# Four more units with states in quarters: a planned stage of an mLSTM and MLP kernel is re-planned

## The chip, the cores and the metric

The kernel runs on one core of a Trainium2 chip. The metric is the time of one execution on the device in microseconds; the median over the runs counts. A profile comes from a separate execution, which has a time of its own.

## The reference, cut to what matters

An mLSTM cell runs over 768 tokens for 4 batches of 8 heads with 40 features each; its output, seen as 3072 tokens of 320 features, goes through an MLP with 2048 hidden units and the activation h - tanh(h).

```python
m_new = np.maximum(f_gate[:, :, t] + m, i_gate[:, :, t])
f_stab = np.exp(f_gate[:, :, t] + m - m_new)
i_stab = np.exp(i_gate[:, :, t] - m_new)
C = f_stab * C + i_stab * einsum('bhd,bhe->bhde', vt, kt)
n = f_stab * n + i_stab * kt
h_tilde = einsum('bhde,bhe->bhd', C, qt)
denom = np.maximum(np.abs(einsum('bhd,bhd->bh', n, qt)), 1.0)
y[:, :, t] = o * h_tilde / denom        # o = sigmoid(o_gate)
...
h = x @ w_in
g = h - np.tanh(h)
return g @ w_out
```

## The kernel before

**Units and items.** The cell's work is cut into 24 units: unit n is 128 tokens (chunk c = n // 4) of batch b = n % 4, all 8 heads. Two units make a group of 256 tokens for the MLP (12 groups). The MLP's hidden units are cut into 8 pairs of 128-wide blocks; (group, pair) is the MLP's step, and an item is two such steps. On TensorE an item has 12 products ph_up (x times w_in) and then, one item later, the products with w_out: either 8 `po` products, or, where the group or the pair is number 4 or later, 7 products per step instead of 8 (`pS`, in `down_seven`; the names "runs of seven products" and "third bank" belong to it). `sums_of_g` and `sums_of_weights` make the sums that the seven products need, and `put_together` adds the results up on VectorE.

**A unit, in trios.** Scores (`ps`) are k times q for each head; the mask makes P of them, on VectorE (TENSOR_TENSOR P) or, for the units in BY_POOL, by a copy on ScalarE and an affine_select on GpSimd. `vs` are the values scaled by the input gate, with a column of the gate itself. `ph` is then the state of the chunk before times q (three products over trios of heads, from a second layout of q, `q2`) plus P times vs (eight products, P as the weights). `gate` divides by the denominator and multiplies by the sigmoid; three transposes on TensorE (`px`) and a copy bring y into `xT`, in which the MLP reads it. `update` (`pc`, three products) and `keep_state` make the new state.

**A unit, in quarters.** Units from 12 on hold the state in two halves of 64 rows. `block_turned` computes the result transposed, P streaming past the values (`pT`: 8 products with the state, 8 with P, into quarters of two banks), and 8 small state products (`pc`, 64x41). The result comes back by a trip through DRAM: `turn_back` transposes 32x32 blocks on VectorE (`zt`), stores them (4 DMAs `h_rows`) and loads them (4 DMAs `z_in`); `gate_turned` makes y; `turn_by_store` transposes blocks again (`yt`), stores (4 DMAs `y_rows`) and loads into xT (2 DMAs). All of these DMAs are on SP's queue. `in_halves` carries a state from trios to halves with small DMAs SBUF to SBUF.

**Weights.** They arrive as float64 bits; `weights` fetches a block with DMAs on GpSimd's queue and converts it: two ops on VectorE (`parts`), two on ScalarE (`low`, `power`), then `one`, `sign` and `product` on VectorE.

**What sets the order.** The class Pinned and T keep each engine's instructions in the order in which the program calls them. For units 0 to 11 and the items up to START this order comes from `Plan`: a list scheduler over engines with estimated durations, buffers as tokens, ranks, earliest times (`at`) and lags; where TensorE would idle, it puts in filler products (`awake`, lines of `stream`). After the plan a loop merges the rest: each item's products with the slots of units 12 to 23. Between the two stands `load_unit(PLANNED, ("kz", "qz", "v", "k", "o"))`, unit 12's loads on SP; in the kernel before, the in_halves of the four batches come right behind it. Line L129 of the profile is the helper that records TensorE's products, L133 its transposes, L106 the helper of all other engines.

Of the kernel before, what the change touches and what calls it, by code (L numbers as in the profile page):

```python
# [60 lines left out]
L = 128  # L61
# [18 lines left out]
def kernel(  # L80
# [76 lines left out]
    class Plan:  # L157
# [5 lines left out]
        COLD, TURN, WAIT = (6.2, 1.8), 0.12, 0.2188  # L163
# [346 lines left out]
    def weights(dst, srcs, queue):  # L510
# [41 lines left out]
        def product():  # L552
            V.tensor_tensor(out=dst, in0=w["r"], in1=w["e"].bitcast(FP), op=OP.mult)
# [5 lines left out]
    def blocks_of(p):  # L559
# [9 lines left out]
        for i in range(2):  # L569
            whole.append((slice(i * HALF, (i + 1) * HALF), slices(4, 1), moe_w_in[half[i]:half[i] + HALF, slices(2 * p + i, 1)]))  # L570
        return (weights(w_in[:, p, :], whole, G),
                weights(w_out[:, 2 * p:2 * p + 2, :].rearrange("p two n -> p (two n)"),
                        [(every, slice(0, 2 * DM), moe_w_out[slices(2 * p, 2), :].rearrange("(two p) n -> p two n", two=2))], G))
# [40 lines left out]
    def scaled(n, i, name, bufs, by_heads=False):  # L614

        t = un[n]
        flat = att.tile([L, H * D1 + HALF - D1], FP, name=name, tag=name, bufs=bufs)
        to = flat[:, 0:H * D1].rearrange("p (h d) -> p h d", d=D1)
        t["wide"] = flat
        scale = ei[:, i, t["c"], t["hs"]]  # L620
        t["column"] = lambda: A.copy(out=to[:, :, D], in_=scale)
        if by_heads:
            for h in range(H):
                A.mul(out=to[:, h, 0:D], in_=t["v"][:, h], mul=scale[:, h:h + 1])
        else:
            V.tensor_tensor(out=to[:, :, 0:D], in0=t["v"], in1=scale.unsqueeze(2).to_broadcast([L, H, D]), op=OP.mult)
        return to
# [107 lines left out]
    def turn_by_store(n):  # L735
# [6 lines left out]
        V.transpose(flat[:, 0:NK * 128], y[:, 0:NK * 128])  # L742
        V.transpose(flat[:, NK * 128:], y[:, FROM[NK]:])
        rows = dram.tile([(NK + 1) * 128, L], FP, name="y_rows", tag=f"y_rows{n % 4}")
        for a in range(L // BLOCK):
            part = slice(a * BLOCK, (a + 1) * BLOCK)
            SP.dma_start(out=rows[:, part].rearrange("(b i) j -> i b j", i=BLOCK), in_=yt[part])
        for i in range(2):
            half = slice(i * HALF, (i + 1) * HALF)
            SP.dma_start(out=xT[g % NX][half, :, tt * L:(tt + 1) * L], in_=rows.rearrange("(c p) t -> p c t", p=128)[half])  # L750

    def in_halves(b):


        old, new = (state[b][i].rearrange("p h d -> p (h d)") for i in (1, 0))
        for h in (0, 1, 2, 4, 5, 6, 7):
            i, j = divmod(h, HH)
            r = h % TRIO
            n = 2 if h == 0 else 1
            to, at = (x[:, first * D1:(first + TRIO * (n - 1) + 1) * D1].rearrange("p (h d) -> p h d", d=D1)[:, ::TRIO]  # L760
                      for x, first in ((new, j), (old, h)))
            SP.dma_start(out=to[i * HALF:i * HALF + D], in_=at[r * D:(r + 1) * D])

    def block_turned(n):
# [4 lines left out]
        G.memset(t["wide"][:, H * D1:], 0.0)  # L769
# [31 lines left out]
    def turn_back(n):  # L801
# [5 lines left out]
        for i in range(2):  # L807
            V.transpose(flat[:, i * 2 * L:(i + 1) * 2 * L], t["turned"][i].rearrange("p g t -> p (g t)"))
        rows = dram.tile([2, 2, HH, L, BLOCK], FP, name="h_rows", tag=f"h_rows{n % 4}")
        for a in range(128 // BLOCK):  # L810
            half, low = divmod(a, 2)
            SP.dma_start(out=rows[low, half].rearrange("g (b k) i -> k (g b) i", k=BLOCK), in_=zt[a * BLOCK:(a + 1) * BLOCK])
        t["z"] = att.tile([L, 2, H, BLOCK], FP, name="z_in", tag="P", bufs=4)
        for i in range(4):
            part = slice(i * BLOCK, (i + 1) * BLOCK)
            SP.dma_start(out=t["z"][part].rearrange("t a h i -> t (a h) i"),
                         in_=rows.rearrange("a c g t i -> t (a c g) i")[part])
# [27 lines left out]
    def cell_slot(s, o):  # L845
# [16 lines left out]
        steps.append((0.0, lambda: turn_by_store(o)))  # L862
# [303 lines left out]
    SCALED, SHARED = (7, 11), (3, 5, 7, 8, 9, 10, 11)  # L1166
    RANKS = (-1.0, -1.0, -8.2006, -8.4463, 6.0242, 2.3893, 9.5327, 2.6415, 25.6922, 13.6176, 29.7021, 7.061)
    WEIGHTS = (0.08, -0.3563, 5.1266, 7.6972, 9.6586, 11.6503, 11.1391, 25.4848)
    START = item(FIRST * NP)
    HOLD = 43.9795  # L1170
    FETCH = {(0, 1): 6.75, (2, 1): 12.25, (3, 0): 19.87, (3, 1): 31.49}
    APART = ()
    BY_POOL = (2, 5, 6, 7, 8, 9)
# [56 lines left out]
    LATE = {"o": -2.69, "k": -3.541, "q2": -4.0692, "v": -1.3038}  # L1230

    def plan_unit(n, rank):
# [17 lines left out]
        else:  # L1250
# [3 lines left out]
            if c:  # L1254
# [14 lines left out]
        u["scores"] = plan.add("T", 1.0, first_part, [u["qz"], *(of(n - 2, "second") if n in (2, 3) else [])], rank, [(bank, held), ("P", held)], tiles=2, hold=HOLD * (n // B), dense=0.4 if n else 0.6)  # L1269
        if n in BY_POOL:  # L1270
            copies = [plan.add("A", 0.55, lambda i=i: ready[1][i][0](), [u["scores"]], rank - 6.4275, give=[(bank, held)] if i else ()) for i in range(2)]
            u["mask"] = [plan.add("G", 0.9, lambda i=i: ready[1][i][1](), [copies[i]], rank + 2.098, lag=0.1) for i in range(2)]
        else:
            u["mask"] = [plan.add("V", 0.62, lambda i=i: ready[1][i](), [u["scores"]], rank - 1.673, give=[(bank, held)] if i else ())
                         for i in range(2)]
        before = of(n - B, "state")
# [4 lines left out]
        op = None  # L1281

        def second_part(j, heads):
            banks[:] = [held["small"]]
            inter(n, j)
            for h in heads:
                intra(n, h)

        parts = TRIOS if c else [range(i * HH, (i + 1) * HH) for i in range(2)]
        for j, heads in enumerate(parts):  # L1290
            op = plan.add("T", 0.223 * len(heads) + (0.22 if c else 0.0), lambda j=j, heads=heads: second_part(j, heads),
                          ([op] if op else [u["prep"], u["column"], *before, *of(n, "q2") * (c > 0)]) + (u["mask"] if c else u["mask"][j:j + 1]), rank,
                          take=() if op else [("small", held)], give=[("P", held)] if j == len(parts) - 1 else (), dense=0.32)
        u["second"] = op
        if shared:
            steps = []
            over = plan.add("V", 0.6, lambda: [steps.extend(gate(n, in_parts=True)), steps[0]()], [op], rank - 0.2851)
            shares = plan.add("A", 1.9, lambda: steps[1](), [over, u["open"]], rank + 9.0221)
            u["gate"] = plan.add("V", 0.5, lambda: steps[2](), [shares, *of(n - 2, "turn")], rank - 7.2476, give=[("small", held)])
        else:  # L1300
            u["gate"] = plan.add("V", 1.6, lambda: gate(n), [op, u["open"], *of(n - 2, "turn")], rank, give=[("small", held)])

# [7 lines left out]
        def turns():  # L1310
            banks[:] = [held_x["small"]]
            for j in range(NK + 1):
                turn(n, j, at_once=False)

        u["turn"] = plan.add("T", 0.35, turns, [u["gate"]], rank, [("small", held_x)], dense=0.5)
        u["x"] = plan.add("A", 0.5, lambda: keep_x(n), [u["turn"]], rank + 1.345, give=[("small", held_x)])
        late = rank + (3.0653 if c else -10.0273)
        u["update"] = plan.add("T", 0.64, updates, [u["second"], u["k"]], late, [("small", held_c)], [("vs", held)],
                               at=0.0 if c else 0.0 if n < 2 else 50.4842, dense=0.5)
        u["state"] = plan.add("V", 1.0 if c else 0.5, lambda: keep_state(n), [u["update"], *before, *of_states[c]], late, give=[("small", held_c)])  # L1320
# [3 lines left out]
    def plan_weights(p, rank, at):  # L1324
        for k, block in enumerate(blocks_of(p)):
            fetch, parts, low, power, one, sign, product = block
            held, r, buffer = {}, rank + 4.428 * k, "w64" + "ab"[k]
# [7 lines left out]
            converted[p, k] = plan.add("V", 0.75, product, [op] + (of_tokens[NT - 1] + of_states[NT - 1] if p >= KEPT else []), r, give=[("w", held)])  # L1335
# [7 lines left out]
    for n in range(2, PLANNED):  # L1343
        if n == 2 * B:
            plan_gates(1, 8.7699, 30.0, in_po)
# [6 lines left out]
    for p in range(SPLIT, NP):  # L1352
        steps = []
        op = None
        for i in range(2):
            op = plan.add("V", 0.65, lambda p=p, i=i, steps=steps: [steps.extend([] if i else sums_of_weights(p)), *[step() for _, step in steps[2 * i:2 * i + 2]]],
                          [op] if op else [converted[p, 1], *([made[p - 1]] if p % 2 else [converted[n, k] for n in range(1, NP) for k in range(2)])], -7.7512 + -3.8283 * p)
        made[p] = op

    def plan_item(x):  # L1360
# [35 lines left out]
        for i in range(2):  # L1396
            z.append(plan.add("A", 0.3 + 0.25 * n, lambda i=i: square(i), [op, *z], -1.1546, () if i else [("z", held), ("gt", held)]))
        q = [plan.add("A", 0.2 + 0.25 * n, lambda i=i: got[2][1](i), [z[i]], -7.0688) for i in range(2)]
        cube = [plan.add("V", 0.15 + 0.27 * n, lambda i=i: got[2][2](i), [z[i]], -8.4237, give=[("up", held)] if i else ()) for i in range(2)]
        g = [plan.add("V", 0.15 + 0.27 * n, lambda i=i: got[2][3](i), [q[i], cube[1]], -17.7698, give=[("z", held)] if i else ()) for i in range(2)]  # L1400
        shrunk = g
        seven, (group, pair) = in_seven(*some[0]), some[0]
        if seven:
            g = [plan.add("V", 0.8 * n, lambda: sums_of_g(some), g[-1:], 4.1746, [("w", held), ("s4", held)])]
# [315 lines left out]
```

## Time and profile before

| what | value |
|---|---|
| median of 3 runs | 521.77 us (521.42, 521.77, 532.6) |
| the profiled execution: time | 523.67 us |
| the profiled execution: span | 522.0 us |
| mean granted TensorE clock | 0.995 |
| TensorE busy | 512.8 us, 98% |
| VectorE, ScalarE, GpSimd busy | 368.4, 200.6, 38.3 us |
| scores of unit 12 begin on TensorE | 209.71 us |

The lines of the profile name an engine (PE is TensorE, DVE VectorE, ACT ScalarE, POOL GpSimd, SPq the queue of SyncE), a line, an operation, what it writes and reads by the program's names, and how often. Times in the timeline and in the chain are microseconds from the start of the span: first the start, then the length of the stretch. In the chain a stretch lasts until the next one begins; in the timeline it lasts until its last instruction's end.

### The profile page before, as it was taken

Reading aid. Unit: us, or ns where it says so; the run is one execution under the profiler, and the core shown is the slowest. Engines: PE = TensorE matmul, PEld = TensorE weight load, DVE = VectorE, ACT = ScalarE, POOL = GpSimd, SP = SyncE. Lnnn points to the kernel's source line nnn. Section 1 sums busy time; section 2 is a strip of 40 time slices with the busy share of each in tenths; the row PEclk is TensorE's granted clock in tenths of the full one; section 3 lists DMA queues with packets and bytes.
Section 4 is the critical chain, followed back from the end, with each engine's and each line's share of the span. In section 5 each row is a group of like instructions: output and inputs, shape, how many; then the busy total and the mean of one; then the engine's idle time right before and its main releaser. Section 6 shows DMA issues by size and latency. Waiting matters only on the chain.

```text
span 522.0 us, 9917 instructions
## 1 busy us (share of the span) xinstructions
PE 512.8 (98%) x3705; PEld 442.4 (85%) x3705; DVE 368.4 (71%) x828; ACT 200.6 (38%) x511; POOL 38.3 (7%) x75
## 2 busy tenths in 40 slices
PE   9999999999999999999999999999999999999995
PEld 5778888887898888898898898898888888898984
DVE  5899979998855657786767667668658658663734
ACT  4465697676434242231321331232232232232321
POOL 5423224120000000000000000000000000000000
PEclk9899999999999999999999999999999999999999
DMA  7987646431003000042533533534433432310001
GB/s 228 285 245 227 180 141 193 131 111 33 3 3 91 6 27 26 4 108 50 133 64 89 147 67 85 129 69 87 107 77 85 107 79 36 80 31 1 26 1 31
DMA packets 100383, 47.29 MB, mean 91 GB/s; under 512 B 75048, under 2 KB 94056, under 8 KB 100328
## 3 DMA queue, kind: packets, MB, share of 16 engines
q1 hardware_dynamic: 94096, 31.84, 25.3%
q0 software_dynamic: 3040, 10.82, 6.6%
q10 hardware_dynamic: 3192, 3.93, 2.2%
q8 instruction: 31, 0.51, 0.4%
q14 instruction: 24, 0.20, 0.1%
HBM read 36.91 MB, written 9.44 MB: 89 GB/s over the span
## 4 chain that ended last, share of the span: by engine, by line
PE 94%; DMA 3%; ACT 1%; POOL 1%; DVE 0%; issue 0%; SPq 0%; DVEq 0%
PE ph_up L129 42%; PE pS L129 31%; PE po L129 7%; PE ph L129 4%; PE pT L129 4%; PE ps L129 4%; PE pc L129 2%; DMA w<-in_moe_w_in 2%; PE px L133 1%; DMA w_out<-in_i_gate 0%; POOL w L106 0%; ACT vs L106 0%; PE awake L129 0%; ACT L106 0%; DVE w_in L106 0%
## 5 line engine op out<-in xcount | busy, mean ns | idle before, releaser
L129 PE MATMUL ph_up<-xT,w_in 128*128 128x256 f32 (+1 forms) x1152 | 228.9, 388 | 0.0
L129 PEld LDWEIGHTS ph_up<-xT,w_in 128*128 128x128 f32 (+1 forms) x1152 | 176.2, 189 | 35.5 <-issue 15.3
L106 ACT ACTIVATE z<-ph_up 128x512 f32<-128x512 f32 (+1 forms) x98 | 56.8, 583 | 254.2 <-issue 123.7
L106 DVE SCALAR_TENSOR_TENSOR gt<-ph_up,z 128x512 f32<-128x512 f32 (+1 forms) x98 | 63.5, 675 | 68.0 <-ACT z L106 67.6
L129 PE MATMUL pS<-wT,s 128*128 128x160 f32 x480 | 72.0, 299 | 0.0
L129 PEld LDWEIGHTS pS<-wT,s 128*128 128x128 f32 x480 | 67.4, 190 | 0.0
L106 ACT ACTIVATE q<-z,tiny 128x512 f32<-128x512 f32 (+1 forms) x98 | 66.3, 711 | 1.0
L106 DVE SCALAR_TENSOR_TENSOR gt<-q,gt 128x512 f32<-128x512 f32 (+1 forms) x98 | 63.2, 676 | 0.0
L106 DVE TENSOR_TENSOR P<-ps,upto 128x512 f32<-128x512 f32 x36 | 23.3, 686 | 52.9 <-PE ps L129 52.8
L129 PE MATMUL pS<-w_out,gt 128*128 128x160 f32 x320 | 54.3, 312 | 0.0
L129 PEld LDWEIGHTS pS<-w_out,gt 128*128 128x128 f32 x320 | 44.6, 189 | 7.5 <-issue 3.6
L129 PE MATMUL po<-w_out,gt 128*128 128x320 f32 x128 | 38.2, 441 | 0.0
L129 PEld LDWEIGHTS po<-w_out,gt 128*128 128x128 f32 x128 | 23.1, 190 | 8.5 <-issue 0.3
L106 DVE TENSOR_TENSOR s<-gt 128x256 f32<-128x256 f32 x80 | 30.2, 418 | 0.0
L129 PE MATMUL pS<-w_out,s 128*128 128x160 f32 x160 | 28.3, 299 | 0.0
L129 PE MATMUL pS<-wT,gt 128*128 128x160 f32 x160 | 28.3, 299 | 0.0
L129 PEld LDWEIGHTS ps<-qz,kz 40*128 40x128 f32 x384 | 25.7, 190 | 2.1 <-issue 0.7
L129 PE MATMUL ps<-qz,kz 40*128 40x128 f32 x384 | 26.5, 276 | 0.0
L129 PEld LDWEIGHTS ph<-vs,P 128*128 128x128 f32 x192 | 23.9, 192 | 1.6 <-POOL P L106 1.2
L129 PE MATMUL ph<-vs,P 128*128 128x41 f32 x192 | 24.4, 273 | 0.7 <-POOL P L106 0.7
L129 PEld LDWEIGHTS pS<-w_out,s 128*128 128x128 f32 x160 | 23.9, 190 | 0.0
L129 PEld LDWEIGHTS pS<-wT,gt 128*128 128x128 f32 x160 | 23.9, 190 | 0.0
(105 smaller groups left out, 475.6 us busy)
## 6 DMA issues: line engine op xcount, KB each, us to landing
w<-in_moe_w_out POOLq DMA_DIRECT2D x8, 640.0 KB, 6.2
w<-in_moe_w_in POOLq DMA_DIRECT2D x16, 256.0 KB, 4.7
kz<-in_kT SPq DMA_DIRECT2D x48, 80.0 KB
o<-in_o_gate SPq DMA_DIRECT2D x24, 160.0 KB
k<-in_k SPq DMA_DIRECT2D x20, 180.0 KB
qz<-in_qT SPq DMA_DIRECT2D x44, 80.0 KB
v<-in_v SPq DMA_DIRECT2D x22, 160.0 KB
out<-ob ACTq DMA_DIRECT2D x11, 320.0 KB
```

The lines of the kernel that those rows point to most:

```text
L106: i = method(*args, **kwargs)
L129: return cls.keep(nc.tensor.matmul(*args, **kwargs))
L133: return cls.keep(nc.tensor.transpose(*args, **kwargs))
```

## The change

Units 8 to 11 (FLIPPED) are also computed in quarters, inside the plan: the trips through memory become steps of the plan (`turn_back` and `turn_by_store` now return three steps, blocks, stores and loads). `in_halves` moves into the plan, before each of these units, and carries eight pieces from state 0 to state 1 instead of seven from 1 to 0. The memset of vs's tail goes from GpSimd to VectorE and is done in `scaled`. Five weight products (ONE_BY_POOL) go to GpSimd. The third bank of the seven-product runs of groups 0 and 2 moves to the small banks (IN_SMALL). All ranks, earliest times, fetch times and the lists SCALED, SHARED, BY_POOL and APART are new. The load of unit 12 stays behind the plan.

```diff
-    def weights(dst, srcs, queue):
+    def weights(dst, srcs, queue, by_pool=False):
...
-            V.tensor_tensor(out=dst, in0=w["r"], in1=w["e"].bitcast(FP), op=OP.mult)
+            (G if by_pool else V).tensor_tensor(out=dst, in0=w["r"], in1=w["e"].bitcast(FP), op=OP.mult)
...
+        if n in FLIPPED or n >= PLANNED:
+            V.memset(flat[:, H * D1:], 0.0)
...
     def in_halves(b):
-        old, new = (state[b][i].rearrange("p h d -> p (h d)") for i in (1, 0))
-        for h in (0, 1, 2, 4, 5, 6, 7):
+        old, new = (state[b][i].rearrange("p h d -> p (h d)") for i in (0, 1))
+        for h in range(H):
...
+            SP.dma_start(out=new[i * HALF:i * HALF + D, j * D1:(j + 1) * D1], in_=old[r * D:(r + 1) * D, h * D1:(h + 1) * D1])
...
     def block_turned(n):
         t = un[n]
-        G.memset(t["wide"][:, H * D1:], 0.0)
...
-    SCALED, SHARED = (7, 11), (3, 5, 7, 8, 9, 10, 11)
+    SCALED, SHARED = (7, 10), (3, 4, 5, 9, 10)
...
-    FETCH = {(0, 1): 6.75, (2, 1): 12.25, (3, 0): 19.87, (3, 1): 31.49}
-    APART = ()
-    BY_POOL = (2, 5, 6, 7, 8, 9)
+    FETCH = {(2, 1): 18.26, (3, 0): 18.54, (3, 1): 38.13}
+    APART = (2,)
+    FLIPPED = (8, 9, 10, 11)
+    FLIPS = (3.0955, -4.5081, 2.7967, 0.1482, -2.8187, -1.6309)
+    SCORED = {4: 26.61, 6: 23.58, 8: 98.4, 9: 133.43, 10: 139.01, 11: 78.31}
+    ONE_BY_POOL = ((0, 1), (2, 1), (3, 0), (5, 1), (6, 1))
+    IN_SMALL = (0, 2, 3)
+    BY_POOL = (2, 5, 6, 9, 11)
...
+        if n in FLIPPED:
+            before = [plan.add("S", 2.8, lambda: in_halves(b), of(n - B, "state"), rank + FLIPS[5])]
+        else:
+            before = of(n - B, "state")
...
+            u["second"] = plan.add("T", 1.9, products, [u["prep"], u["column"], *u["mask"], u["k"], *before], rank + FLIPS[0], [("a", banked), ("small", held_c)], [("P", held), ("vs", held)], tiles=3, dense=0.9)
+            blocks = plan.add("V", 0.75, lambda: [backs.extend(turn_back(n)), backs[0]()], [u["second"]], rank + FLIPS[1], [("P", turned)], [("a", banked)])
+            u["update"] = u["state"] = plan.add("V", 0.5, lambda: keep_halves(n), [u["second"], *of_states[c]], rank + FLIPS[2], give=[("small", held_c)])
+            stores = plan.add("S", 2.1, lambda: backs[1](), [blocks], rank - 0.5, give=[("P", turned)])
+            loads = u["loads"] = plan.add("S", 2.1, lambda: backs[2](), [stores], rank - 0.5, [("P", back)])
+            both = plan.add("V", 1.0, lambda: [gates.extend(gate_turned(n)), *[step() for step in gates[:2]]], [loads, u["open"], *of(n - 2, "turn")], rank + FLIPS[3])
+            u["gate"] = plan.add("V", 0.6, lambda: [step() for step in gates[2:]], [both], rank + FLIPS[3], give=[("P", back)])
+            u["turn"] = plan.add("V", 0.65, lambda: [turns_y.extend(turn_by_store(n)), turns_y[0]()], [u["gate"]], rank + FLIPS[4])
+            stores = plan.add("S", 2.1, lambda: turns_y[1](), [u["turn"]], rank - 0.5)
+            u["x"] = plan.add("S", 1.3, lambda: turns_y[2](), [stores], rank - 0.5)
...
-            name = "small" if group == FIRST - 1 else "a"
+            name = "small" if group in IN_SMALL else "a"
...
+    plan.add("T", 0.0, lambda: None, [units[n]["x"] for n in (FIRST * GT, FIRST * GT + 1)], 1000.0)
...
     load_unit(PLANNED, ("kz", "qz", "v", "k", "o"))
-    for b in range(B):
-        in_halves(b)
```

## The prediction, made before the changed kernel was run

> **What bounds the kernel now.** I read the page first: how full TensorE is, and whose time the chain that ended last consists of.
>
> ```profile
> span 522.0 us, 9917 instructions
> PE 512.8 (98%) x3705; PEld 442.4 (85%) x3705; DVE 368.4 (71%) x828; ACT 200.6 (38%) x511; POOL 38.3 (7%) x75
> ...
> PE 94%; DMA 3%; ACT 1%; POOL 1%; DVE 0%; issue 0%; SPq 0%; DVEq 0%
> ```
>
> TensorE is the bound, and nearly nothing else is on the path. So two things count: how many microseconds of products the change takes off TensorE, and whether it makes TensorE wait. For the first I read the chain in order of time (start, duration, what). Fp32 products have two records each, transposes one.
>
> ```profile
> 56.94 0.65 PE px L133 x6
> ...
> 130.52 1.72 PE ph L129 x16
> ...
> 133.18 0.60 PE ph L129 x6
> 133.77 0.67 PE pc L129 x6
> ...
> 205.19 4.52 PE ph_up L129 x24
> 209.71 0.89 PE ps L129 x16
> 210.60 4.00 PE pS L129 x28
> ...
> 219.12 1.62 PE pT L129 x32
> 221.19 4.00 PE pS L129 x28
> ```
>
> The three rows from 130 us are unit 11 as it is now; the row at 56.94 is the turning of two units' results. A unit in quarters (from 219.12) has its block products and then its small state products until the next row at 221.19: 2.07 us. Between 205 and 215 one sees that TensorE goes from one group to the next without a gap: the scores of unit 12 start at 209.71, the moment the 24 records before them end.
>
> For the second I read the queue that a unit in quarters needs, SP's issues in order of time, which stand behind each other in one order:
>
> ```profile
> 164.53 0.87 SPq L106 DMA_DIRECT2D kz<-in_kT  x2
> ...
> 225.63 1.98 SPq L106 DMA_DIRECT2D h_rows<-zt  x4
> 229.09 1.90 SPq L106 DMA_DIRECT2D z_in<-h_rows  x4
> 231.03 0.80 SPq L106 DMA_DIRECT2D kz<-in_kT  x2
> 231.88 0.69 SPq L106 DMA_DIRECT2D qz<-in_qT  x2
> ...
> 242.04 1.90 SPq L106 DMA_DIRECT2D y_rows<-yt  x4
> 245.40 1.35 SPq L106 DMA_DIRECT2D xT<-y_rows  x2
> 246.86 2.20 SPq L106 DMA_DIRECT2D h_rows<-zt  x4
> ```
>
> Unit 12's keys and queries are issued at 164.53, 45 us before their use. Unit 13's, at 231.03, already stand behind unit 12's first trip through memory (h_rows, z_in). VectorE's part of such a trip, start and duration:
>
> ```profile
> 236.29 0.16 DVE L106 SCALAR_TENSOR_TENSOR den<-z_in,inv 128x8 f32<-128x8 f32 x1
> ...
> 241.37 0.64 DVE L106 STREAM_TRANSPOSE yt<-ys 128x256 f32<-128x256 f32 x2
> ```
>
> Last, the granted clock in windows (us, PE busy, clock, DMA share, GB/s):
>
> ```profile
> 18.82:22.23 3.41, 2.70 (x21) 1.00 0.94 276
> 22.23:25.64 3.41, 3.41 (x16) 0.50 0.75 246
> ```
>
> A stretch of 3.41 us in which TensorE was busy for 2.70 us is followed by one at half the clock, then full again.
>
> **Products removed.** Units 8 to 11 now: ph and pc rows 2.98 us (99.90), 2.91 (110.01), 2.99 (130.52) and 2.98 (148.48), plus half of 0.65 each for turning: 11.86 + 1.30 = 13.16 us. In quarters they take 4 x 2.07 = 8.28 us. That is 4.88 us less. One filler product more (awake) costs 0.22: net -4.66 us, all of it before unit 12's scores, which would therefore start at about 205.0.
>
> **The wait added.** In the changed program SP's queue holds, one after the other: unit 10's y_rows and xT, unit 11's h_rows, z_in, y_rows and xT, and only then kz and qz of unit 12 (load_unit(PLANNED) stands behind the whole plan). On TensorE unit 11's block products are followed by one item's 24 ph_up and then by unit 12's scores. Before, unit 11 put nothing on SP behind its loads. Count from the end of the 24 ph_up ahead of unit 11's own scores:
> - Unit 10's yt ends at 3.6 us: two Squares and their reads come first, but VectorE's first gt then (0.69), a memset (0.10), vs (0.48), ys (0.42 + 0.22), yt (0.64) make 2.55 behind the sums of the item before, which end about 1.05 after.
> - y_rows to the end of xT took 242.04 to 246.76, 4.72 us: 8.3. Unit 11's h_rows start at 8.4 (0.1 behind xT, as at 246.86). Its zt is done by 7.9.
> - h_rows to z_in: 225.63 to 229.09, later 3.68; I take 3.6: 12.0.
> - z_in: 1.90 of issue and a landing. h_rows landed 1.47 after their last issue (227.62 to 229.09). 15.4.
> - den to yt: five operations 236.29 to 237.88, ys 0.22, yt 0.64: 2.45. With queue 17.9.
> - y_rows and xT again 4.72: 22.6.
> - kz and qz: 231.03 to 232.57 is 1.54 of issue; the DMA share falls from 0.68 to 0.04 within 1.8 us of the last load's issue (o, 234.21), so 1.8 to land: 26.0.
> TensorE gets there at 0.89 + 4.00 + 2.07 + 4.52 = 11.48. The wait is 14.5 us. Nothing on TensorE can go ahead of it; behind it stand all later items. On ScalarE the column and the sigmoid of unit 12 wait for v and o, and the Squares of the running item stand behind them; o lands 1.3 us after qz, and the banks that these Squares free are due 0.89 + 4.00 us after the scores begin, so this adds nothing. Bounds: z_in and load landings 0.3 shorter and h_rows going out 0.9 earlier give 12.9; h_rows in its slow form (266.77 to z_in at 271.68, 4.91 us) and y_rows at 5.17 give 16.3.
>
> **The clock.** [...] In the window at 22.23 the rows pc 1.09, ph_up 1.78 and ps 1.41 stood for 0.64, 0.92 and 0.89: 1.83 us lost in 3.41. [...] If the clock did not fall it would be 0.
>
> [...]
>
> **Edits at nothing.** VectorE gains per unit two zt (0.77), yt (0.7) and smaller state sums, and gives up five weight products of 0.84; the cover is its idle time (over 160 to 205 us it is busy for 29.6 of 45), and without it each us would be one of TensorE's. in_halves puts 32 small issues on SP behind the states of units 4 to 7, where 28 stood from 121 us on. Unit 8's eight need 8 x 0.45 + 1.8 = 5.4 us; in the order 44 ph_up (16.6 us) and 30 po (16.9 us) lie between unit 4's state and unit 8's block. Moving third banks leaves 4.52 us of ph_up for 2.9 us of put_together: cover 1.6 us, and each us beyond it would be one us of TensorE.
>
> GpSimd has no two-input product in this trace. affine_select on 128x512 took 852 ns, so 640 elements take 1.07 at least and, reading two inputs, 2.0 at most; I take 1.5. The tightest is w_out of pair 0: VectorE's w_e ends at 33.05 and the po that reads it starts at 36.01, so even 2.0 is covered by 0.9. The next fetch goes from 33.35 to at most 35.1, and its use is a pair later. Cost 0; with the cover gone, at most 2.0 each, 10 in all, of which half might show.
>
> [...]
>
> **Sum.** Profiled execution: 523.67 (span 522.0 and 1.67 around it) - 4.66 + 14.5 + 2.4 = 535.9. It is 1.9 above the median of the runs, as much as one window at half clock costs; the median is my base: 521.77 + 12.2 = 534.0.
>
> **Rivals.**
> - *No wait*: unit 12's loads are there in time, only the saving is left: 517.1. For it: unit 12's loads now come 45 us early, and later units hide theirs. Against: the queue's order, and no buffer or engine that would let kz pass unit 11's trip. Place: unit 12's scores. It decides while wait and clock together stay under 4.66 us, that is, if kz is issued at about 12 instead of 22.6. Ends on the not slower side.
> - *Wait without the clock*: the granted clock stays full: 531.6, within 2%. Against it: 18.82 to 25.64.
> - *GpSimd's products collide with VectorE too*: VectorE is at 9 tenths up to some 70 us; half of 10 us shows: 539.0.
> - *The change doesn't save the products*: units 8 to 11 cost as before, 538.7; against it stand the same rows in units 12 to 23.
>
> **How the numbers follow.** Forecast 0.75, with its own 531.5 to 537. No wait 0.09. Wait without the clock 0.08. Collisions 0.06. No saving 0.02. The range, 530 to 539, goes from the shortest wait with a full clock (521.77 - 4.66 + 12.9 = 530.0) to the longest with the worst clock and 2 us of collisions (538.7); it leaves out the case without a wait and the tails. 2% (532.2 and 511.3) is about what a measurement of this kernel can tell from no change. Slower: nearly all of the forecast and the last two, 0.79. Within 2%: no wait, full clock and the forecast's low end, 0.19. Faster by over 2% would need 10 us off TensorE: 0.02.
>
> **What would show it.** Right: pT x32 four times more, before unit 12; on TensorE a gap of 13 to 16 us ahead of one ps, near 205 us, put down to the landing of qz; in the page's slices one with a low PE digit and PEclk below 9 there; in SP's issues kz directly behind xT at about 216 us; ph_up at doubled durations for 3 to 6 us. Wrong: ps following ph_up without a gap, kz ahead of unit 11's h_rows, or gaps of a microsecond scattered before 140 us behind GpSimd's products.

## The result, and the profile after

| kernel | median | times |
|---|---|---|
| before | 521.69 us | 521.25 to 521.80, and one of 532.60 |
| changed | 542.37 us | 537.78, 537.95, 539.38, 545.36, 546.08, 546.72 |

The changed kernel is slower: ratio 1.036, 95% interval 1.028 to 1.043. Some runs of either kernel take 8 to 11 us more than its others, three of these six among them, so the change is to be read from the group near 538.

The page of the changed kernel, profiled in a run of 546.08 us: span, the busy times, TensorE's slices and granted clock, and the shares of the chain that ended last.

```profile
span 544.4 us, 10118 instructions
PE 520.7 (96%) x3774; PEld 444.8 (82%) x3774; DVE 371.6 (68%) x865; ACT 190.3 (35%) x473; POOL 42.2 (8%) x66
...
PE   9999999999999997099999999999999999999996
...
PEclk9999999999999999589999999999999999999999
...
PE 89%; DMA 3%; SPq 3%; DVE 2%; ACT 2%; issue 1%; DVEq 0%; ACTq 0%
```

TensorE has one empty slice (the 17th), the clock is low there and after it, and SP, DMA and VectorE are on the chain, which before was 94% TensorE. The clock row does not show the start: that its record begins at 30.4 us, and that the rows before it have double durations (ps 2.08 us for 1.16), only the timeline tells.

TensorE's timeline there (start, length, what; in brackets the idle time ahead and what ended it):

```profile
197.31 4.68 PE L129 MATMUL ph_up<-xT,w_in 128*128 128x256 f32 x24
201.83 1.06 PE L129 MATMUL ps<-qz,kz 40*128 40x128 f32 x16
...
206.82 0.67 PE L129 MATMUL pT<-qz,state 40*64 40x128 f32 x16
207.42 1.09 PE L129 MATMUL pT<-P,vs 128*64 128x128 f32 x16
...
208.89 4.79 PE L129 MATMUL ph_up<-xT,w_in 128*128 128x256 f32 x24
230.23 2.62 PE L129 MATMUL ps<-qz,kz 40*128 40x128 f32 x16 [16.56 <-DMA qz<-in_qT]
232.78 2.50 PE L129 MATMUL pS<-w_out,gt 128*128 128x160 f32 x8
```

Unit 11 now has its pT rows, and unit 12's scores, which followed the 24 ph_up without a gap before, wait 16.56 us for qz. SP's issues say why:

```profile
205.45 1.85 SPq L106 DMA_DIRECT2D y_rows<-yt  x4
210.48 1.24 SPq L106 DMA_DIRECT2D xT<-y_rows  x2
211.84 2.14 SPq L106 DMA_DIRECT2D h_rows<-zt  x4
215.57 1.90 SPq L106 DMA_DIRECT2D z_in<-h_rows  x4
221.67 1.86 SPq L106 DMA_DIRECT2D y_rows<-yt  x4
225.03 1.24 SPq L106 DMA_DIRECT2D xT<-y_rows  x2
226.31 0.90 SPq L106 DMA_DIRECT2D kz<-in_kT  x2
227.25 0.71 SPq L106 DMA_DIRECT2D qz<-in_qT  x2
```

kz stands behind unit 10's return and unit 11's whole trip, in the order that the prediction listed. The granted clock in windows (from:to, length, then the busy time of TensorE, its weight loads, VectorE, ScalarE and GpSimd, then the clock, the DMA share and GB/s):

```profile
218.12:230.20 12.08, 0.00 (x0) 0.00 (x0) 3.26 (x13) 0.00 (x0) 0.00 (x0) 0.50 0.35 84
230.20:235.19 4.99, 4.96 (x25) 4.69 (x26) 3.15 (x8) 2.53 (x7) 0.00 (x0) 0.50 0.73 227
235.19:238.60 3.41, 3.41 (x25) 3.33 (x24) 3.27 (x8) 0.61 (x2) 0.00 (x0) 1.00 0.00 0
```

The clock falls 4.5 us into the idle stretch and comes back 5.0 us after the restart. From ps to the next 24 ph_up it takes 237.85 - 230.23 = 7.62 us where it took 214.44 - 209.71 = 4.73: 2.9 us lost. The half clock, 0.50 in these rows, accounts by my estimate for half of those 5.0 us, 2.5.

### The profile page after: what moved, and what is told of

It is laid out like the page before. It is cut to its first block, busy times and chain, and to the rows that moved or that the text cites. A ratio compares the mean times of both kernels' runs of the same rounds, so it can differ in the third digit from the quotient of the medians.

```text
span 544.4 us, 10118 instructions
## 1 busy us (share of the span) xinstructions
PE 520.7 (96%) x3774; PEld 444.8 (82%) x3774; DVE 371.6 (68%) x865; ACT 190.3 (35%) x473; POOL 42.2 (8%) x66
## 4 chain that ended last, share of the span: by engine, by line
PE 89%; DMA 3%; SPq 3%; DVE 2%; ACT 2%; issue 1%; DVEq 0%; ACTq 0%
PE ph_up L129 38%; PE pS L129 29%; PE po L129 6%; PE ps L129 5%; PE pT L129 4%; PE awake L129 3%; PE ph L129 3%; SPq L106 3%; PE pc L129 1%; DMA y_rows<-yt 1%; PE px L133 1%; DMA qz<-in_qT 1%; DMA k<-in_k 0%; DMA z_in<-h_rows 0%; ACT z L106 0%
## 5 line engine op out<-in xcount | busy, mean ns | idle before, releaser
L106 DVE TENSOR_TENSOR P<-ps,upto 128x512 f32<-128x512 f32 x38 | 24.6, 684 | 54.1 <-PE ps L129 54.1
L129 PE MATMUL pS<-w_out,gt 128*128 128x160 f32 x320 | 55.5, 317 | 0.0
L129 PE MATMUL ps<-qz,kz 40*128 40x128 f32 x384 | 30.1, 300 | 16.6 <-DMA qz<-in_qT 16.6
L129 PEld LDWEIGHTS ps<-qz,kz 40*128 40x128 f32 x384 | 28.7, 210 | 19.2 <-issue 17.3
L106 POOL DMA_DIRECT2D w<-in_moe_w_in x32 | 18.5, 585 | 30.5 <-DVE w_e L106 26.8
L106 ACT ACTIVATE o<-o 128x320 f32<-128x320 f32 x24 | 11.3, 470 | 26.4 <-DMA o<-in_o_gate 26.3
```

The source lines that it names most:

```text
L106: i = method(*args, **kwargs)
L129: return cls.keep(nc.tensor.matmul(*args, **kwargs))
```

## The experiments

"The best kernel" in an expectation is the one that the later of the two put-off runs gave. A distance that serves throughout is that from the first row of 24 ph_up to the row of 24 ph_up ahead of unit 12's scores: 166.86 us before (38.17 to 205.03), 162.20 in the changed kernel (46.69 to 208.89).

**The changed kernel again** (no edit).

> The changed kernel itself once more, for a profile whose start is like that of the kernel before, and for more of its times. My theory: TensorE's end of the 24 ph_up ahead of unit 11's scores lies 4.7 to 5.3 us earlier than in the kernel before, the wait ahead of unit 12's scores is 16.3 to 16.7 us, half clock costs 1.9 to 2.9 us behind it, and undisturbed runs end near 521.6 - 4.7 + 16.5 + 2.4 = 535.8, at most 538. Rival (the change itself makes the start slower): the first units' products come 2 us or more later than in the undisturbed profiles of its own variants, in most runs.

Median 537.74 us (537.10 to 538.43, and one of 545.79), ratio 1.028 (1.024 to 1.033); profiled in a run of 538.43 us, span 536.7. Two of TensorE's waits there (who <- whom: us in all, times, the longest):

```profile
PE ps L129 <- DMA kz<-in_kT: 16.5, 1, 16.5
PE ph L129 <- POOL P L106: 1.2, 1, 1.2
```

The distance is 162.17 us: 4.69 less than before. The wait is 16.53, and ps to the next 24 ph_up takes 7.93 us, 3.2 more than before (2.9 at most expected; 5.6 us at half clock, from 222.18 to 227.80, make 2.8 of it). The start is 0.5 us later (38.69 for 38.17; a wait for P, 1.2 us for 0.7), not 2. This profile and that of the kernel before both have 3.41 us at half clock near 23 us. The parts nearly add up to the span: 522.0 + 0.5 - 4.7 + 16.5 + 3.2 - 1.0 = 536.5. The last term is the stretch from that 24 ph_up behind unit 12's scores to the end of the span, 306.6 us here and 307.6 before; nothing that I ran says why.

**Unit 12's loads early.**

```diff
-            loads = u["loads"] = plan.add("S", 2.1, lambda: backs[2](), ...
+            loads = u["loads"] = plan.add("S", 2.1, lambda: [backs[2](), n == 10 and load_unit(PLANNED, ("kz", "qz", "v", "k", "o"))], ...
...
-    load_unit(PLANNED, ("kz", "qz", "v", "k", "o"))
```

> The changed kernel with one edit: unit 12's five loads are issued on SP right behind unit 10's z_in instead of behind the whole plan. My theory (the wait is the queue's order and nothing else): no gap ahead of unit 12's scores (under 0.5 us instead of 16.6), no half clock there, so 16.7 + 1.9 us less than the changed kernel: 517.0 if all else is as in the kernel before (521.7 - 4.7), up to 519.5 if the 2.4 us that I can't place in the changed kernel's time stay. Rival A (TensorE would wait for something else there, such as xT, v or o, so the loads only hide another wait): a gap of 5 us or more stays, 523 to 530. Rival B (the changed kernel loses at the start of the program, by a clock that rises later): the gap goes, but the time is 520 to 525.

Median 528.50 us (525.33 to 534.59), ratio 1.012 (1.007 to 1.018); span 523.6 in the profiled run. The scores of unit 12 follow without a gap, as I expected, but rival A was right on the rest: another wait stands behind, one group later. The waits of TensorE and of VectorE, then VectorE's timeline:

```profile
PE ph_up L129 <- DVE gt L106: 7.5, 1, 7.5
...
DVE den L106 <- DMA z_in<-h_rows: 9.0, 1, 9.0
```

```profile
207.96 0.17 DVE L106 SCALAR_TENSOR_TENSOR den<-z_in,inv 128x8 f32<-128x8 f32 x1 [8.99 <-DMA z_in<-h_rows]
...
209.80 0.64 DVE L106 STREAM_TRANSPOSE yt<-ys 128x256 f32<-128x256 f32 x2
...
211.80 1.28 DVE L106 TENSOR_TENSOR P<-ps,upto 128x512 f32<-128x512 f32 x2
...
214.07 1.28 DVE L106 SCALAR_TENSOR_TENSOR gt<-ph_up,z 128x512 f32<-128x512 f32 x2
```

Unit 11's den is the first instruction on VectorE behind a trip that has not landed, and the plan put nothing between. VectorE stands for 9 us; behind it are unit 12's P and the gt that free the banks of ph_up. So TensorE stops at 207.4, one group later than in the changed kernel. In the changed kernel the same 9.0 us are there, hidden under the longer wait for kz and qz. A half clock of 4.0 us after the restart (214.90 to 218.90, clock 0.50) costs another 2.0 us, by my estimate half of it.

**The loads in the middle.** kz and qz behind unit 11's z_in (in the same line with n == 11), v, k and o left.

> The changed kernel with kz and qz of unit 12 issued behind unit 11's z_in, ahead of its y_rows; v, k and o stay behind the plan. My theory: kz is issued when z_in's issues end, 8.8 us earlier than in the changed kernel, so the wait ahead of unit 12's scores is 16.6 - 8.8 = 7.8 us, and the time 8.8 us less than the changed kernel's (529 where that has 537.8), with nearly the whole loss of clock (1.5 to 1.9 us) kept, since 7.8 us of idle time is still longer than two windows of 3.41. Rival A (another wait stands behind): the gap stays at 12 us or more. If the clock's loss goes by the length of the idle time: 1.0 us less again.

Median 531.81 us (529.87 to 532.80), ratio 1.019 (1.017 to 1.021). TensorE waits 6.91 us for qz (7.8 expected), then 3.22 us more for VectorE's gt:

```profile
209.58 2.45 PE L129 MATMUL ps<-qz,kz 40*128 40x128 f32 x16 [6.91 <-DMA qz<-in_qT]
...
221.40 2.83 PE L129 MATMUL ph_up<-xT,w_in 128*128 128x256 f32 x12 [3.22 <-DVE gt L106]
```

The first wait goes with the place of kz on SP's queue, so the queue's order is its cause. The second I had not expected when I wrote this. VectorE's timeline says where it comes from: gt stands behind vs, and vs waits for v, which was left behind unit 11's y_rows and xT on SP (issued at 215.37).

```profile
217.90 0.49 DVE L106 TENSOR_TENSOR vs<-v,ei 128x320 f32<-128x320 f32 x1 [6.16 <-DMA v<-in_v]
```

The clock's loss did not shrink with the idle time: it stays at half for 6.8 us behind the restart after 6.9 us of idleness, against 5.0 and 5.6 after 16.5. That the loss would be kept because the idle time is longer than two windows of 3.41 us was my estimate; the runs show these lengths and not why.

```profile
209.50:216.37 6.87, 6.79 (x32) 6.60 (x33) 2.17 (x9) 0.00 (x0) 0.00 (x0) 0.50 0.26 50
```

**Fillers during the wait.**

```diff
+    def before_scores(rest, new):
+        if PLANNED in new:
+            for step in rest[0]:
+                step()
+            stream(ps_a.tile([128, 512], FP, name="awake", tag="a0"), 72)
+            rest = ([], rest[1])
+        halves(rest, *(scores(n) for n in new))
...
-            dense.append((0.6 + 0.9 * len(new[:1]), lambda: halves(rest, *(scores(n) for n in new[:1]))))
+            dense.append((0.6 + 0.9 * len(new[:1]), lambda: before_scores(rest, new[:1])))
```

> The changed kernel with 72 filler products (72 x 0.217 = 15.6 us) ahead of unit 12's scores, where TensorE waits for qz. My theory: the scores begin when they began before, the granted clock stays 1.00 through the wait, the rows ps and pS behind it take 0.89 and 4.00 instead of 2.62 and 5.16, and the time is 1.9 us less than the changed kernel's (535.9 where that has 537.8). Rival (the clock falls for another reason than TensorE's idle time): half clock after the wait as before, no gain.

Median 534.12 us (533.45 to 536.43), ratio 1.025 (1.022 to 1.027). In windows:

```profile
202.70:218.40 15.70, 15.70 (x74) 6.96 (x72) 3.27 (x13) 0.00 (x0) 0.00 (x0) 1.00 0.35 68
218.40:219.50 1.10, 0.07 (x2) 0.06 (x1) 0.00 (x0) 0.00 (x0) 0.00 (x0) 1.00 0.84 263
219.50:226.00 6.50, 6.48 (x50) 6.07 (x51) 5.09 (x12) 3.03 (x8) 0.00 (x0) 1.00 0.60 182
```

The clock stays at 1.00, and ps to the next 24 ph_up takes 224.91 - 219.47 = 5.44 us. Of its 7.93 us in the changed kernel's second profile 2.5 are gone, more than the 1.9 that I expected; by the medians the time is 3.6 us less (534.12 for 537.74). 0.7 us over the 4.73 before stay at full clock, 0.5 of them in the row of the scores (1.60 us for 1.06), which seem to wait for the second half of qz. So here the half clock comes from TensorE's idleness: 0.50 behind the idle wait, 1.00 with the wait filled.

**The five weight products back on VectorE** (`product` always on V, the rest as it is).

> The changed kernel with the five weight products back on VectorE, the order of all engines else as it is. My theory: they cost nothing on GpSimd, so 0 to 0.5 us either way against the changed kernel, the wait ahead of unit 12's scores the same 16.6 us. Rival (GpSimd's products hold up VectorE or the products that read the weights): 2 to 5 us less than the changed kernel, and small gaps on TensorE before 100 us gone.

Median 536.98 us (536.45 to 537.47, and one of 546.19), ratio 1.029 (1.027 to 1.030). The distance is 162.31 us (36.23 to 198.54) against 162.17, and the wait 16.3; the median is 0.8 us under the changed kernel's, where I gave 0.5, with intervals that overlap. The tightest of the products, w_out of pair 0, lies ahead of that distance: there the rows from px to the first 24 ph_up take 11.81 us (26.88 to 38.69, the changed kernel's second profile) for 11.82 before (26.35 to 38.17). On GpSimd the products are longer than I took (1.5 us), but nobody waits for them (the changed kernel's first profile: busy us, mean ns, then GpSimd's own idle time ahead):

```profile
L106 POOL TENSOR_TENSOR w_out<-w_r,w_e 128x640 f32<-128x640 f32 x4 | 6.6, 1658 | 26.5 <-DVE w_e L106 18.3 <-issue 8.2
L106 POOL TENSOR_TENSOR w_in<-w_r,w_e 128x640 f32<-128x640 f32 x1 | 1.9, 1913 | 4.0 <-DVE w_e L106 4.0
```

**Both waits away.** The loads early, and unit 11's den to yt (VectorE), y_rows and xT (SP) put off into the next item: first behind its gt<-ph_up, then further, behind its gt<-q and its sums.

```diff
+    def put_off(n, step):
+        return step if n < PLANNED - 1 else lambda: late_steps.append(step)
...
-            u["turn"] = plan.add("V", 0.65, lambda: [turns_y.extend(turn_by_store(n)), turns_y[0]()], ...
+            u["turn"] = plan.add("V", 0.65, put_off(n, lambda: [turns_y.extend(turn_by_store(n)), turns_y[0]()]), ...
...
+    spread_over([(0.0, lambda: [step() for step in late_steps])], START + 0.8, START + 1.0)
```

`both`, `gate`, `stores` and `x` are wrapped in the same way; the later place has 0.95 for 0.8.

> Unit 12's loads early as in the run with early loads, and unit 11's gates and its return (den to yt on VectorE, y_rows and xT on SP) put off until behind the two gt<-ph_up of the next item. My theory (two waits, one behind the other, on the same trip through memory: unit 12's loads on SP, and behind them the gt that stand behind unit 11's den on VectorE): no gap over 1 us on TensorE between 190 and 225 us, no half clock there, and the time of the kernel before less the products saved and 0.6 us for the lighter VectorE: 516 to 517.5. Rival (a third wait stands behind the second, or den's wait moves on to the next item's gt): 519 to 523 and a gap of 2 us or more before 240 us.

Median 517.53 us, the lowest 516.86, at the upper end of what I gave; ratio 0.991 (0.988 to 0.994). No half clock between 6 and 514 us (mean granted clock 0.999). One wait of about 1 us is left, for the adding up of a group (ob) that comes behind den:

```profile
PE pS L129 <- DVE ob L106: 1.1, 1, 1.1
```

> The same with unit 11's gates and return put off further, behind the next item's second gt, its sums and the adding up of group 3's results. My theory: den comes when z_in has long landed, so VectorE waits nowhere; 516 to 517.5 again, and at most 1 us better than the nearer place. Rival (unit 12's own trip, whose h_rows stand behind unit 11's y_rows and xT on SP, comes too late by it): a new gap on TensorE one or two items later, 518 to 522.

Median 516.77 us, the lowest 516.11; ratio 0.991 (0.988 to 0.995). The scores of unit 12, pS and the next ph_up stand in one row again:

```profile
198.44 4.79 PE L129 MATMUL ph_up<-xT,w_in 128*128 128x256 f32 x24
203.06 1.06 PE L129 MATMUL ps<-qz,kz 40*128 40x128 f32 x16
...
207.96 4.68 PE L129 MATMUL ph_up<-xT,w_in 128*128 128x256 f32 x24
```

On VectorE gt comes at 206.41 and den, without a wait, at 210.47. This is the fastest kernel of this study, 5.7 us under the kernel before by the medians of this comparison (522.47) and 4.6 by the ratio, which is about the price of the products taken off. Between the two places the times differ by 0.8 us, too little against their intervals.

**Put off, but the loads behind the plan.**

> Unit 11's gates and return put off as in the later place, but unit 12's loads left behind the whole plan. On SP kz of unit 12 then stands right behind unit 11's z_in, without y_rows and xT between them, and on VectorE nothing stands behind den. My theory (two waits that add up): the first wait is that of the run with the loads in the middle, 6.9 us; the second, 3.2 us there, is gone; the half clock costs 2.0 to 3.4 us. From the best kernel's 516.8 that makes 516.8 + 6.9 + 2.7 = 526.4, 525.5 to 527.2. Rival (the two waits are one, so that the put-off alone takes both away): 517 to 520. Rival (the second wait comes from the loads on SP and not from VectorE's queue): a gap ahead of the next ph_up stays, 529 or more.

Median 527.77 us (527.11 to 530.82), ratio 1.011 (1.003 to 1.018): 0.6 us outside what I gave. One wait is left, of 8.12 us, and the next 24 ph_up follow without a gap (two lines of TensorE's timeline, one of VectorE's):

```profile
211.76 2.70 PE L129 MATMUL ps<-qz,kz 40*128 40x128 f32 x16 [8.12 <-DMA qz<-in_qT]
219.69 4.68 PE L129 MATMUL ph_up<-xT,w_in 128*128 128x256 f32 x24
212.56 0.49 DVE L106 TENSOR_TENSOR vs<-v,ei 128x320 f32<-128x320 f32 x1 [11.36 <-DMA v<-in_v]
```

So the put-off takes away the second wait and not the first. It does not decide between the theory and the last rival: with y_rows and xT put off, v too comes sooner on SP (209.30 for 215.37 with the loads in the middle), and vs, whose wait for v held up gt there, starts at 212.56 for 217.90. That den on VectorE is a wait of its own is shown by the runs with the loads early, where v had landed: 7.5 us with den in its place, 1.1 and none with den put off. The first wait is 1.2 us longer than with the loads in the middle, with kz at the same place on the queue; 0.8 us of that lie between kz's issue and the scores (207.71 to 211.76 for 206.36 to 209.58). In this kernel v, k, o and unit 13's loads are issued right behind qz, from 209.30 on, before qz has landed; that their traffic is the reason was not tried.

## Why the prediction was wrong

**The direction and the mechanism held.** TensorE's distance became 4.69 us shorter; 4.66 were forecast. The wait is at the place, behind the queue and on the transfer that were named, and moving the loads moves it. The clock falls in it (0.50 from 218.12 to 235.19 us in the first profile), and with fillers it does not (1.00). The edits costed at nothing cost nothing that can be seen by the distance and the rows ahead of it, the GpSimd products among them.

**The base failed, by 5 to 6 us.** The sum was set on the median of the runs before, as if the start were the same in all runs. In the changed kernel's first profile the start alone costs 8.5 us: its rows are at about double length, as at half clock, up to 30.4 us, and its first row of 24 ph_up comes at 46.69 us for 38.17 before.

```profile
11.22 2.08 PE L129 MATMUL ps<-qz,kz 40*128 40x128 f32 x16
46.69 4.68 PE L129 MATMUL ph_up<-xT,w_in 128*128 128x256 f32 x24
```

The same rows in its second profile:

```profile
8.85 1.16 PE L129 MATMUL ps<-qz,kz 40*128 40x128 f32 x16
38.69 4.68 PE L129 MATMUL ph_up<-xT,w_in 128*128 128x256 f32 x24
```

Three of the six times are longer than the other three by about that much, and the median, 542.37, lies between. With the measured terms the sum is 521.8 - 4.7 + 16.5 + 3.0 = 536.6, about 1 us under the three shorter ones. The counts do not show that the change makes such a start more frequent: 4 of the changed kernel's 12 times and 16 of the 49 of the kernel before are 5 us or more above the fastest. That all of these start in the same way was not profiled, and why the start differs stays open.

**The wait was 2.0 to 2.1 us too short**, 14.5 for 16.5 to 16.6. By its steps, from the same point (the end of the 24 ph_up at 202.05):

| step | predicted | measured |
|---|---|---|
| unit 10's yt ends | 3.6 | 3.4 |
| xT ends | 8.3 | 9.7 |
| unit 11's z_in issued | 12.0 | 13.5 |
| z_in landed | 15.4 | 17.0 |
| unit 11's yt ends | 17.9 | 19.6 |
| xT ends | 22.6 | 24.2 |
| unit 12's scores begin | 26.0 | 28.2 |

The step that failed first is "y_rows to the end of xT took 242.04 to 246.76, 4.72 us": unit 10's took 6.27, unit 11's, "y_rows and xT again 4.72", 4.6. The chain of waits shows y_rows on its way for 3.52 us there and for 1.86 us sixteen microseconds later (what goes with it stands in the last section):

```profile
206.83 3.52 DMA y_rows<-yt
...
223.05 1.86 DMA y_rows<-yt
```

The second is the landing of the loads: from the end of qz's issue to the first product 2.3 us, not 1.8. The upper bound of 16.3, too, was exceeded: it gave this step 5.17 at the most and put the rest on h_rows, which were not late (3.73 us to z_in for 3.6).

**The clock's term came out near its size**: 2.5 and 2.8 us for 2.4. From ps to the next 24 ph_up 2.9 and 3.2 us were lost; half of the 5.0 and 5.6 us at half clock are 2.5 and 2.8. The other 0.4 us is not the clock's, since with fillers 0.7 us are lost at full clock too; the sum had no term for it.

No run shows what the term of 2.4 us in the sum would follow from. What the runs show is half clock for 4.0 to 6.8 us behind the restart, where 3 to 6 us were looked for: 4.0 with the loads early, 5.0 and 5.6 in the changed kernel's two profiles, 5.5 with the put-off alone, 6.3 with the products back on VectorE, 6.8 with the loads in the middle. Half of these stretches is 2.0 to 3.4 us, so it is in part luck that the size fits. In the first profile the half clock from 218.12 to 235.19 us is 17.07 us, five times the 3.41 that it lasted in the kernel before (22.23 to 25.64), and all six values lie between one and two times 3.41.

In five of the six waits TensorE was busy for 0.03 us at the most in the 3.41 us ahead of the clock's fall; with the products back on VectorE it was busy for 1.34 us in them, and the next stretch already had half clock.

```profile
201.99:205.40 3.41, 1.34 (x10) 0.69 (x8) 0.00 (x0) 0.00 (x0) 0.00 (x0) 1.00 0.58 112
205.40:219.50 14.10, 0.00 (x0) 0.00 (x0) 3.27 (x13) 0.00 (x0) 0.00 (x0) 0.50 0.36 78
```

No threshold comes out of these runs: 3.41 us busy for 1.73 us (203.91 to 207.32, the changed kernel's second profile) and 3.41 us busy for 2.16 us (205.25 to 208.66, the loads early) were followed by full clock, while the prediction's row at 18.82, busy for 2.70 us, was followed by half clock.

**What the prediction missed altogether** is the second wait. I asked what stands behind kz on SP and behind the late loads on ScalarE, and not what stands behind den on VectorE, whose z_in I had in the sum as a step. It costs nothing while the first wait covers it. But the rival "no wait" was said to be decided by the place of kz alone, and with kz early the profiled run had 525.3 us and not 517.1: the gt that TensorE waits for stood behind den, which waited 9.0 us for z_in. Only with both waits away did the time come to 516.8.

**GpSimd's duration** was taken as 1.5 us and is 1.66 for w_out and 1.91 for w_in, where VectorE takes 0.82 (the kernel with the products back on VectorE); the cover held.

## What to carry to other kernels

Here VectorE stood for 9.0 us at den, which reads the result of a trip through memory, and with it P and gt, which the plan puts behind that read; TensorE waited 16.5 us for loads that stood behind unit 10's return and unit 11's trip on SP. List for each queue and each engine what stands behind such a read, not only for the one whose wait ends last. When a wait is removed, look under it for the next one before the whole gain is booked. A planned stretch that ends in a trip needs its successor's loads and its own late steps laid across the seam; here two small moves turned 16 us lost into about 5 us won.

## What the runs showed of the hardware

**Stores of small packets landed late where a fetch of instructions fell into them.** The 4 DMAs y_rows write 1536 packets of 128 bytes. xT, which waits for them, was issued either 1.3 to 1.6 us after the last of them (113 trips) or 2.4 to 3.5 us after it (43), nothing between. In all ten profiles of this study every late one has a 16 KB packet of the instruction queue (q8) that begins 1.7 to 3.2 us after the first y_rows was issued, and of the others none (three of them have one within the first 0.5 us). The DMA view of such a trip (from 197.40 to 202.30 us, the changed kernel's second profile) counts it (packets, MB, share of 16 engines' time):

```profile
q1 hardware_dynamic: 1600, 0.20, 26.9%
q8 instruction: 1, 0.02, 1.4%
```

Such a packet took 0.9 to 1.5 us; in the first profile (207.88 to 209.29) 23 of the 1536 packets started only after it. The same trip (unit 10's) was hit in the changed kernel and in all its variants, so the place goes with the program. I only saw these two things together and did not move the fetch to test it.

**The start ran as at half clock in one profile, long after TensorE was busy.** In the first profile of the changed kernel TensorE was busy nearly without a gap from 1.1 us on, and its rows are at about double length until 30.4 us (ps 2.08 us at 6.06); in the second the clock is full from 5.9 us on (ps 1.16 us at 6.11), but for the 3.41 us near 23 us. Nothing in the program differs between the two.
